# A two-branch sequence mixer on one core: the opening (input transposes, small vector loads, first TensorE work) and the step list are changed

## Chip, cores and metric

One core of a Trainium2 chip. The metric is the device time of one execution in microseconds: the median of the runs of the kernel. Durations below come from one profiled execution of the kernel before the change.

## What is computed

`x` is 2048 rows of 512. Two branches are computed from it and mixed by a gate per row.

```python
g = sigmoid((x * gate_w).sum(-1, keepdims=True))

# a: a diagonal complex state-space recurrence
dt = exp(log_dt);  Lam_bar = exp(dt * Lam);  B_bar = ((Lam_bar - 1) / Lam)[:, None] * Bmat
Bu = einsum("bld,pd->blp", x, B_bar)
h[t] = Lam_bar * h[t-1] + Bu[t]
a = 2 * einsum("blp,dp->bld", h, Cmat).real + x * Dskip

# b: linear attention with softmax features, 32 heads of 16
q, k, v = split(x @ wqkv)
phi(u) = concat(softmax(u @ w_phi), softmax(-u @ w_phi))
kv = sum_s phi(k)[s] v[s];  z = sum_s phi(k)[s]
b = (phi(q) kv) / (phi(q) z + 1e-6) @ wo

out = g * a + (1 - g) * b
```

## The kernel before

**The step list.** Each piece of work is a Python generator named by a short token, and every `yield` ends a part of it. The string `ORDER` (lines 24 to 53) is read token by token (lines 752 to 757): each token runs its generator up to the next `yield`. So `ORDER` is the order of instructions on TensorE, VectorE and ScalarE and of the late transfers on SyncE; each engine runs its own in that order and waits at the head of its list. `@5` names the PSUM bank that the part takes, `:D` gives an eviction to VectorE instead of ScalarE.

**The opening.** ScalarE's queue issues the load of the natural `Wk` block into `wk_nat` (the tile is named `C2r`, line 156), then `Wc` (157), then `Wv` (161). SyncE's queue issues five loads of 1 KB into the rows of `vec_n` (Lambda_im, Lambda_re, log_dt, Dskip, gate_w; line 159), then transposing loads of x tiles 0 to 7 (`x_load`, line 221), `Bn_r` and `Bn_i` (225, 226), eight transposing loads of `BrT`, `BiT` (228, 229), x tiles 8 to 15 and more. A DMA can be held at its issue by the landing of an earlier one.

**Steps that the prediction speaks of.** `W0` to `W3` (line 270) transpose `wk_nat` on TensorE and evict it; `f0` to `f3` (fold, line 372) multiply it with the block-diagonal `BD` made from `Wc` by `B` (305); each `f` reads all four `W`. `V` (278) transposes `vec_n` and copies it into `vec`, and GpSimd makes the diagonal `Dd` from its Dskip. `U`, `P`, `P2`, `P3`, `P4` work out the recurrence's magnitudes and angles from `vec` on VectorE and ScalarE; `i0` to `i3` (386) make sine and cosine tables `T2s`, `T2c` from them, with the temporaries `kk` and `psi` in the pool `tabtmp` (two buffers). `M` and `D` make the coefficient diagonals `dg`. `k`, `v`, `q` (418 to 436) are four products of 512 columns for one x tile each. `x`, `n`, `e`, `s` (features of two tiles: maximum, minimum, exponential, sum) run mostly on VectorE; `a0` to `a7` (507) add phi(k) times v into two PSUM banks and, with `gw_b` from `gw`, the gate's sum. `p`, `g`, `z`, `c`, `h`, `K` build the recurrence. At the end `X`, `N`, `E`, `S` make phi(q) for four tiles each and transpose it by DMA into `phT` (501), `o` (687) multiplies it with the summed state and sends `on` through a DMA transpose to `oT` (713), `y` (666) makes the recurrent output, and `t` (716) adds the projection, scales and stores it.

Of the kernel before, what the change touches and what calls it, by code (L numbers as in the profile page):

```python
# [10 lines left out]
ALU = mybir.AluOpType  # L11
AX = mybir.AxisListType
ACT = mybir.ActivationFunctionType
F32 = mybir.dt.float32
BF16 = mybir.dt.bfloat16
# [5 lines left out]
P = 128  # L21
MAGIC = 12582912.0
Z_MAX = 70.0
ORDER = """
B B W0@0 B V@1 V P W3@2 P W0:D W1@3 P2 W2@4 P2 P2 P2 U B W3 P2 gw P3 W1 W2 v1@5 U f1@6 P4 f2@7 P P4 P4 P2 f1 f0@1 P3
i0 U f2 f3@2 v0@0 i0 i1 f0 f3 i1 i0 i0 U i0 i2 i1 i1 v2@3 i2 i1 k2@4 i2 i3 k2 i2 k0@6 i3 k1@7 k1 i2 k0:D v0:D i3 M
v1:D x0 n0 n0 k3@1 k4@2 k5@4 i3 v2 k6@6 n0 k3 i3 v3@0 x0 x0 L x0 k7@7 k5 k4 D n0 x0 n0 v3 p20@5 p02@3 n1 x1 p00@1 e0
k6:D v7@4 p00 p20:D x1 n1 x1 v4@2 p32@0 x1 p22@6 x1 x2 v7 e0 x2 p10@1 p30@5 p12@4 s0 n1 v4 p10 s0 x2 p02 v6@2 p30 s0
x2 n1 v5@1 p22 p32 s0 g000@3 g101@5 n1 n2 s0 p12:D k8@6 k7 s0 e1 e1 k9@0 n2 x2 s0 k8 k9 g101 a0@74 n2 n2 x3 n2 g001@6
k11@0 e2 x3 s1 x3 n3 a0 x3 v6 v10@2 s1 n3 s1 e2 k11 n3 s1 g000 k12@0 D n3 g001 x3 s1 x4 s1 n3 g101 k13@5 k12 s1 n4 s2  # L30
s2 n4 x4 e3 a1 g000 x4 v5 n4 e3 x4 s2 g100@0 a1 n4 g011@3 s2 x4 k13 s2 s3 g100 s2 k10@1 n4 w1@5 g011 s2 g001 k10 s3 s3
a2 n5 n5 w0@6 x5 g100 w1 g010@1 e4 s3 n5 x5 s3 n5 g011 x5 x5 w2@0 s3 D v10 e4 s3 a2 k14@5 x5 g110@2 x6 g011 w0 g010
k15@3 w3@6 n5 a3 n6 s4 g010 k14 w2 e5 s4 v8@5 x6 s4 s4 g010 x6 a3 g111@0 v9@1 e5 z0 k15 s4 x6 g111 s4 g110 v9 c03@3
g110 s5 z0 v8 g201@1 g111 n6 c03 g111 c10@5 n6 n6 s4 a4 x6 g211@3 c02@0 w3 g110 c10 g210@6 z0 s5 z0 n6 g200@2 c13@5 z0
c02 n7 z0 e6 z0 q1@0 s5 z0 x7 s5 e6 x7 q1 g200 a4 n7 s5 c13 q0@0 n7 g201 x7 n7 x7 s5 v14@5 s6 x7 z1 g200 q0 v11@2 g201
z1 s5 q3@0 z1 s6 g210 q3 n7 z0 nA s6 z1 e7 s6 nA v11 c12@1 c12 z0 a5 v14 q2@0 xA z1 z1 xA e7 s7 s6 g210 c01@2 g211
c11@1 xA a5 g210 g211 v12@5 g211 s6 c11 z1 v13@6 z1 nA z2 xA z1 c01 z2 v13 nA s7 s6 g300@3 v12 g301@1 q11@2 z1 xA
c00@6 q2 c00 z2 g300 a6 nA eA xB xB eA s7 v15@5 s7 g311@0 g301 z2 xB g301 nB z2 g311 s7 g300 q7@6 s7 nB sA sA z2 a6
g310@1 g311 q15@3 nB q7 v15 g310 xB s7 xB nB a7 r0 g311 nB q11 g310 z2 sA g310 z3 eB z3 sA eB a7 z3 q5@6 q10@5 z3 q4@0
q15 q6@2 sA Y q8@1 sB h00@3 Y q10 sA z2 q5 h01@5 h00 h10@6 h01 h11@7 q9@3 sB q6 h11 z3 r1 sB q9 z2 q12@5 z3 h10 z2  # L40
q13@2 z3 z3 sA q4 sB z3 K1@7 G h20@3 sB sA r0 sB z3 h31@6 sB sA sA G q13 h20 h21@0 h31 h30@2 h21 Y q12 b0 r1 K0@3 sB
sB sB h30 END o0@6 K1 X1 K0 o0 Y N1 q8 y1@4 X1 o0@0 o0 o2@5 o2 X1 N1 q14@2 X1 o2@7 N1 b0 o0 N1 X1 q14 N1 X2 o1@3 o0 N2
b1 o1 y0@1 o0 G E1 o2 o2 K3@2 o1@6 b1 E1 G y0 N2 o1 r2 X2 o1 E1 E1 o1 K3 K2@0 X2 y1 o0 y0 o2 o3@3 o3 o3@5 y2@2 o3 t0
N2 o1 y2 o3 o1 N2 y3@6 S1 r3 X2 r3 S1 S1 K2 S1 y1 y2 S1 y4@0 X2 S1 o2 t1 o2 N2 o3 S1 y6@7 S1 y7@3 b2 y3 S1 r2 S1 X3 y4
E2 o3 b3 t2 N3 E2 t0 y4 E2 t1 y3 o4@1 E2 X3 b3 y6 y5@5 o3 S2 t2 S2 X3 S2 S2 o4 t0 o4@4 y7 o4 o4 y5 o4 o4 t1 o5@2 t2 o5
S1 X3 o5@1 o5 S1 t3 S2 N3 y7 y5 b2 S2 o5 y11@4 o5 t3 N3 o5 S2 N3 o6@2 o6 o6@6 o4 o5 o6 y6 o7@1 y11 S2 t4 S2 o6 o6 o7
t3 o6 o7@2 X3 y8@6 o7 o7 o6 t4 N3 E3 t5 o7 o7 y9@0 o8@1 y8 t4 o7 E3 t5:D y10@2 S2 E3 S2 o8 S2 o8@5 o8 o8 y9 t6 y11 o8
o8 E3 S3 o9@1 S3 o9 o9@5 t7 o9 t6 t6 o9 y9 t7 S3 S3 o9 o8 y14@7 o9 S3 y8 S3 o10@3 S3 o9 S3 o10 y10 y14 o10@1 t8 o10
o11@5 t5 S3 o10 o10 o11 t9 t8 t7 t9 o11@3 y14 o12@6 o12 o11 o10 S3 y12@1 o12@0 o11 o12 o12 o11 o12 y10 o10 S3 o13@5 S3
o11 o13 o12 y12 o13@6 t10 o13 y15@3 o11 o14@0 o13 t10:D y12 o14 o14@2 o13 y13@5 o14 y15 o12 o13 o15@6 o14 o14 t8 o15  # L50
o13 o15@0 o15 t11 o14 o15 y13 o14 t10 o15 t11 y15 o15 y13 t14 t11 o15 t13 t9 t14 t13:D t12 t12:D t14 t15 t15 t13 t12
t15
"""
TWO_PI_LO = float(np.nextafter(np.float32(2.0 * np.pi), np.float32(0.0)))
INV_2PI = float(1.0 / (2.0 * np.pi))
ACT_SET = "natural_log_exp_and_others"
# [9 lines left out]
def kernel(  # L66
# [18 lines left out]
    nc = tc.nc  # L85
# [13 lines left out]
    x2 = A_x[0]  # L99
# [9 lines left out]
    def bank(shape, dtype, name):  # L109
        return ps.tile(shape, dtype, tag=f"t{sel['banks'].pop(0)}", name=name, bufs=1)  # L110

    def evac(out_ap, in_ap):
        if sel["eng"] == "act":
            nc.scalar.copy(out=out_ap, in_=in_ap)  # L114
        else:
            nc.vector.tensor_copy(out=out_ap, in_=in_ap)
# [31 lines left out]

    man_g = tc.manual_schedule(engines={mybir.EngineType.PE, mybir.EngineType.DVE, mybir.EngineType.Activation, mybir.EngineType.SP})
    man_g.__enter__()  # L150
    vec_n = const.tile([20, P], BF16, name="vec_n")
    Wc = const.tile([P, HG, Dh], BF16, name="Wc")
    Wv = const.tile([P, KT, D], BF16, name="Wv")
    wk_nat = const.tile([P, KT, D], BF16, name="C2r")
    C2r = wk_nat
    nc.scalar.dma_start(out=wk_nat[:], in_=B_wqkv[:, D:2 * D].rearrange("(k p) n -> p k n", p=P))
    nc.scalar.dma_start(out=Wc[:], in_=B_w_phi.rearrange("(k hl) e f -> (hl e) k f", hl=8))
    for n, src in enumerate((A_Lambda_im, A_Lambda_re, A_log_dt, A_Dskip, gate_w)):
        nc.sync.dma_start(out=vec_n[4 * n:4 * n + 4, :], in_=src.rearrange("(j p) -> j p", p=P))
    pin_act_set()  # L160
    nc.scalar.dma_start(out=Wv[:], in_=B_wqkv[:, 2 * D:3 * D].rearrange("(k p) n -> p k n", p=P))

    xT = const.tile([P, KT, S], BF16, name="xT")
    Wo = const.tile([P, KT, D], BF16, name="Wo")
# [9 lines left out]
    RG = const.tile([P, NTI], F32, name="RG")  # L174
    ge = const.tile([P, NTI], F32, name="ge")
    hpi_t = const.tile([P, 1], F32, name="hpi_t")
    nc.vector.memset(hpi_t[:], float(np.pi / 2.0))
    C2i = const.tile([P, PT, D], BF16, name="C2i")
    C3r, C3i = Wk2, Wv
# [40 lines left out]
    def x_load(ti):  # L220
        nc.sync.dma_start_transpose(out=xT[:, :, ti * P:(ti + 1) * P], in_=x_res[ti // 4, ti % 4])

    for ti in range(8):
        x_load(ti)
    nc.sync.dma_start(out=Bn_r[:], in_=A_B_re.rearrange("(j p) d -> p j d", p=P))
    nc.sync.dma_start(out=Bn_i[:], in_=A_B_im.rearrange("(j p) d -> p j d", p=P))
    for kt in range(KT):
# [12 lines left out]
    fk = fk_g.__enter__()  # L240
    sk_g = tc.tile_pool(name="smallK", bufs=1, reuse_waits="tile")
    sk = sk_g.__enter__()
    tab_g = tc.tile_pool(name="tabtmp", bufs=2, reuse_waits="tile")
    tabp = tab_g.__enter__()
    iot = tabp.tile([P, NC], F32, name="iot", bufs=1)
    make_identity(nc, ident[:])
# [29 lines left out]
        yield  # L276

    def st_V():
        pvt = bank([P, 20], BF16, "pvt")
        nc.tensor.transpose(pvt[:], vec_n[:], ident[0:20, 0:20])  # L280
        yield
        nc.vector.tensor_copy(out=vec[:].rearrange("p n j -> p (n j)"), in_=pvt[:])
        nc.gpsimd.affine_select(out=Dd[:], in_=dsk.unsqueeze(2).to_broadcast([P, KT, P]), compare_op=ALU.is_equal,
                                fill=0.0, base=0, pattern=[[0, KT], [-1, P]], channel_multiplier=1)
        yield

    def st_U():
        VT(out=sq2, in0=lam, in1=lam, op=ALU.mult)
        yield
        VT(out=den_, in0=par[:, 4, :], in1=par[:, 5, :], op=ALU.add)  # L290
        yield
        nc.vector.reciprocal(out=den_, in_=den_)
        yield
        VS(out=den_, in0=den_, scalar1=2.0, scalar2=None, op0=ALU.mult)
        yield
# [43 lines left out]
    def st_gw():  # L339
        nc.vector.tensor_copy(out=gw_b[:], in_=vec[:, 4, :])  # L340
        yield
# [208 lines left out]

    def st_c(dst, j):
        d_, da, db = ((C2r, DG_BR, DG_NBI), (C2i, DG_NBI, DG_NBR))[dst]
        pc = bank([P, D], F32, "pc")
        MM(out=pc[:], lhsT=dg[:, da, j, :], rhs=CrT[:, j, :], start=True, stop=False)
        MM(out=pc[:], lhsT=dg[:, db, j, :], rhs=CiT[:, j, :], start=False, stop=True)
        yield
        evac(d_[:, j, :], pc[:])
        yield
# [33 lines left out]
    def st_h(j, ri):  # L592
        U1 = uv[j][:, 0]
        prev = slice(ZP - 1, ZP - 1 + NC)
        da, db = ((DG_MR, DG_NMI), (DG_MI, DG_MR))[ri]
        ph = bank([P, NC], F32, "ph")
        MM(out=ph[:], lhsT=ident[:], rhs=U1[:, ri, :], start=True, stop=False)
        MM(out=ph[:], lhsT=dg[:, da, j, :], rhs=H3[:, j, 0, prev], start=False, stop=False)
        MM(out=ph[:], lhsT=dg[:, db, j, :], rhs=H3[:, j, 1, prev], start=False, stop=True)
        yield  # L600
        evac(H1[:, j, ri, :], ph[:])
        yield

    def st_G():
# [111 lines left out]
    def st_t(n):  # L716
# [8 lines left out]
        else:  # L725
# [4 lines left out]

    small1, big1 = (lambda: sk), (lambda: fk)
    small3, big3 = (lambda: pools["sq"][1]), (lambda: pools["eq"][1])
    st = {"V": st_V(), "U": st_U(), "P": st_P(), "P2": st_P2(), "P3": st_P3(), "P4": st_P4(), "B": st_B(), "gw": st_gw(),
          "M": st_M(), "D": st_D(), "L": st_L(), "G": st_G(), "Y": st_Y(), "END": st_END()}
    for j in range(4):
        st.update({f"W{j}": st_W(j), f"f{j}": st_f(j), f"w{j}": st_w(j), f"i{j}": st_i(j), f"z{j}": st_z(j), f"r{j}": st_r(j),
# [54 lines left out]
```

## Time and profile before

| what | us |
| --- | --- |
| runs shown | 173.09, 172.84, 173.07 |
| median | 173.07 |
| profiled execution, its own time | 173.42 |
| its span in the profile | 171.7 |
| TensorE busy, 1049 products | 157.8 |
| VectorE busy | 144.2 |
| ScalarE busy | 116.9 |
| first transpose of `W` (waits for `wk_nat`) | 4.74 |
| `V` on TensorE / copy to `vec` on VectorE | 5.57 / 5.78 |
| first table pass `i0` on VectorE | 8.86 |
| first product of `v` | 8.96 |
| first product of `k` | 14.35 |

The span runs from the first to the last recorded instruction; the execution's own time has 1.7 us more around it. Busy time of TensorE counts products that overlap in its pipeline, so the pace is read from the distances between starts. In a timeline line the columns are start, duration, engine, line, operation, output from input, shapes and count; several like instructions are merged into one. In a windows line they are the stretch, its length, busy time and count of each engine, granted clock, the DMA engines' share and GB/s.

### The profile page before, as it was taken

What the parts mean: (1) busy time and instruction counts of PE and PEld (TensorE: products, weight loads), DVE (VectorE), ACT (ScalarE), POOL (GpSimd) and SP (SyncE); (2) the same over time, 40 slices, a digit from 0 to 9 for tenths busy, and PEclk for the clock granted to TensorE, in tenths of its full rate; (3) what the DMA queues carried; (4) which work ended last, traced back from release to release, by engine and by line L of the source; (5) the groups of instructions that cost most, each with busy time, mean ns of one, the idle gap of its engine ahead of it and who ended that gap; (6) DMA issues with size and microseconds to landing.
All of it is one profiled execution on the core that took longest, in us unless ns stands there. A gap on an engine that the chain in (4) does not pass through costs nothing.

```text
span 171.7 us, 2969 instructions
## 1 busy us (share of the span) xinstructions
PE 157.8 (92%) x1049; PEld 80.5 (47%) x1069; DVE 144.2 (84%) x349; ACT 116.9 (68%) x239; POOL 5.3 (3%) x23
## 2 busy tenths in 40 slices
PE   0599989999999999999999999999999998998991
PEld 0354456455455454444545444545455543444540
DVE  3775999999999999999999999999999958335411
ACT  2559799988789587586687698896864394251311
POOL 3223000000000000000000000000000000000000
PEclk9999999999999999999999999999999999999999
DMA  5945974554546000000000008341178458596443
GB/s 126 208 106 157 265 96 92 95 116 100 92 95 164 20 0 2 0 4 0 0 0 4 0 0 168 76 33 34 33 183 203 85 145 183 134 174 154 122 138 106
DMA packets 50710, 15.94 MB, mean 93 GB/s; under 512 B 46088, under 2 KB 50696, under 8 KB 50696
## 3 DMA queue, kind: packets, MB, share of 16 engines
q1 hardware_dynamic: 49112, 14.70, 39.9%
q10 hardware_dynamic: 1584, 1.07, 2.6%
q8 instruction: 8, 0.13, 0.3%
q14 instruction: 6, 0.05, 0.1%
HBM read 2.64 MB, written 2.10 MB: 28 GB/s over the span
## 4 chain that ended last, share of the span: by engine, by line
PE 63%; DVE 18%; DMA 11%; ACT 3%; SPq 2%; issue 1%
PE pq L415 8%; PE py L675 6%; PE py L676 6%; PE py L720 6%; PE pgq L538 6%; PE pgq L541 6%; PE pv L415 5%; DMA phT<-EEq 4%; DVE smk L450 3%; DVE mxk L450 3%; PE py L682 2%; DMA xT<-in_A_x_dram 2%; DVE mnk L450 2%; DMA C2r<-in_B_wqkv_dram 2%; PE pk L645 2%; DMA oT<-on 2%
## 5 line engine op out<-in xcount | busy, mean ns | idle before, releaser
L415 PEld LDWEIGHTS <-xT 128*128 128x128 bf16 x192 | 18.4, 99 | 22.7 <-DMA xT<-in_A_x_dram 2.1
L133 ACT ACTIVATE EEk<-EEk 128x1024 bf16<-128x1024 bf16 x20 | 20.9, 1072 | 2.5 <-DVE EEk L466 2.5
L707 DVE SCALAR_TENSOR_TENSOR on<-pn,RG,rd 128x256 bf16<-128x256 f32 x32 | 14.4, 478 | 9.2 <-ACT rd L133 9.2
L133 ACT ACTIVATE ld<-pn 128x16 f32<-128x16 f32 x32 | 5.5, 185 | 18.4 <-PE pn L698 18.1
L415 PE MATMUL pv<-Wv,xT 128*128 128x512 bf16 x62 | 16.3, 400 | 1.9 <-DMA xT<-in_A_x_dram 1.8
L541 PE MATMUL pgq<-xT,LBT 128*128 128x512 bf16 x63 | 16.0, 379 | 0.1
L720 PE MATMUL py<-Wo,oT 128*128 128x512 bf16 x61 | 15.6, 379 | 0.2
L415 PE MATMUL pq<-Wq,xT 128*128 128x512 bf16 x63 | 15.2, 379 | 0.1
L415 PE MATMUL pk<-Wk,xT 128*128 128x512 bf16 x63 | 15.2, 379 | 0.1
L133 ACT ACTIVATE EEq<-EEq 128x1024 bf16<-128x1024 bf16 x12 | 12.2, 1047 | 1.3 <-DVE EEq L466 1.3
L676 PE MATMUL py<-Wv,H 128*128 128x512 bf16 x32 | 12.1, 379 | 0.1
L114 ACT CAST uv<-pgq 128x512 bf16<-128x512 f32 x16 | 9.3, 582 | 3.9 <-PE pgq L546 2.8
L724 ACT ACTIVATE ot<-py,G 128x512 bf16<-128x512 f32 x12 | 8.2, 682 | 5.5 <-PE py L720 4.9
L676 PE MATMUL py<-C2i,H 128*128 128x512 bf16 x31 | 11.7, 379 | 0.1
L675 PE MATMUL py<-C2r,H 128*128 128x512 bf16 x31 | 11.7, 379 | 0.1
L675 PE MATMUL py<-Wk,H 128*128 128x512 bf16 x31 | 11.7, 378 | 0.0
L114 ACT CAST Xq<-pq 128x512 bf16<-128x512 f32 x16 | 9.3, 589 | 3.4 <-PE pq L415 3.3
L698 PEld LDWEIGHTS <-phT 128*128 128x128 bf16 x128 | 7.0, 98 | 7.1 <-DMA phT<-EEq 2.7
L450 DVE TENSOR_TENSOR smk<-smk 128x512 bf16<-128x512 bf16 (+2 forms) x30 | 9.9, 330 | 0.2
L486 DVE TENSOR_TENSOR EEk<-EEk,rck 128x2048 bf16<-128x2048 bf16 x8 | 9.7, 1218 | 0.0
L541 PEld LDWEIGHTS <-LBT 128*128 128x128 bf16 x64 | 6.2, 98 | 7.3
L579 DVE TENSOR_TENSOR_SCAN w<-ssm_par,ut 128x512 bf16<-128x512 f32 x8 | 9.6, 1215 | 0.0
(169 smaller groups left out, 339.4 us busy)
## 6 DMA issues: line engine op xcount, KB each, us to landing
out_dram<-ot SPq DMA_DIRECT2D x16, 128.0 KB, 2.1
C2r<-in_B_wqkv_dram ACTq DMA_DIRECT2D x1, 512.0 KB, 3.9
Wv<-in_B_wqkv_dram ACTq DMA_DIRECT2D x1, 512.0 KB
Bn_r<-in_A_B_re_dram SPq DMA_DIRECT2D x1, 512.0 KB, 4.6
Bn_i<-in_A_B_im_dram SPq DMA_DIRECT2D x1, 512.0 KB
Wo<-in_B_wo_dram SPq DMA_DIRECT2D x1, 512.0 KB
xT<-in_A_x_dram SPq DMA_TRANSPOSE x16, 3.5
oT<-on SPq DMA_TRANSPOSE x16, 2.3
```

The lines of the kernel that those rows point to most:

```text
L114: nc.scalar.copy(out=out_ap, in_=in_ap)
L133: ins = nc.scalar.activation(**kw)
L415: MM(out=pt[:], lhsT=xT[:, kt, ti * P:(ti + 1) * P], rhs=W[:, kt, :], start=(kt == 0), stop=(kt == KT - 1))
L450: VT(out=t[:], in0=cur[:, :, :, 0:n, :], in1=cur[:, :, :, n:2 * n, :], op=op)
L486: VT(out=E5, in0=E5, in1=rc[:].to_broadcast([P, L, 2 * NB, Dh, 4]), op=ALU.mult)
L538: MM(out=pgq[:], lhsT=BT[:, kt, js], rhs=xT[:, kt, r1 * NC:(r1 + 1) * NC], start=(kt == 0), stop=False)
L541: MM(out=pgq[:], lhsT=LBT_[:, kt, js], rhs=xT[:, kt, (r1 - 1) * NC:r1 * NC], start=False, stop=(r1 == 1 and kt == KT - 1))
L579: nc.vector.tensor_tensor_scan(out=w[:, ri, :], data0=rb, data1=ut[:, ri, :], initial=0.0, op0=ALU.mult, op1=ALU.add)
L675: MM(out=py[:], lhsT=src[:, j, 0, off:off + P], rhs=cr[:, j, :], start=(j == 0), stop=False)
L676: MM(out=py[:], lhsT=src[:, j, 1, off:off + P], rhs=ci[:, j, :], start=False, stop=False)
L707: nc.vector.scalar_tensor_tensor(out=on[:, 2 * hf:2 * hf + 2].rearrange("p g h e -> p (g h) e"), in0=pns[hf][:, :, 0:Dh], scalar=RG[:, ti: ...
L720: MM(out=py[:], lhsT=oT[:, g, :], rhs=Wo[:, g, :], start=False, stop=(g == HG - 1))
```

## The change

SyncE's queue opens with the eight x transposes; the vector loads leave it. Lambda_im, Lambda_re and log_dt go to ScalarE's queue, behind `Wk` and ahead of `Wc` and `Wv`, into a tile of 12 rows; Dskip and gate_w go into a tile of 8 rows, loaded by SyncE behind x tile 7. `V` is split to match: `V` for the first three, `V2` for the other two and `Dd`. TensorE opens with nine products of 128x512 of a tile `fillw` that VectorE fills with ones; their bank (`t7`) is read by nobody. `tabtmp` has three buffers instead of two. `ORDER` is another list of the same tokens plus two `V2`. Two options, `C2_VECTOR` and `H1_VECTOR`, are added empty, so they change nothing.

```diff
 ORDER = """
-B B W0@0 B V@1 V P W3@2 P W0:D W1@3 P2 W2@4 P2 P2 P2 U B W3 P2 gw P3 W1 W2 v1@5 U f1@6 P4 f2@7 P P4 P4 P2 f1 f0@1 P3
-i0 U f2 f3@2 v0@0 i0 i1 f0 f3 i1 i0 i0 U i0 i2 i1 i1 v2@3 i2 i1 k2@4 i2 i3 k2 i2 k0@6 i3 k1@7 k1 i2 k0:D v0:D i3 M
...
+V@0 W1@1 V B U P P W1 P2 P2 P W0@2 W2@3 B P2 P2 W3@4 W3 P2 B v2@5 P4 P4 W0:D P4 P3 v1@6 W2 i0 B U P2 f0@7 P3 i2 f1@0
+f3@1 U i1 f2@4 f0 i0 f3 f1 i2 f2 U i0 v3@3 i0 i1 v5@2 i0 i1 k1@7 v3:D M i1 k1 k0@1 i1 i2 k2@0 i2 k0:D k5@4 i3 v4@3 v1
...
-    vec_n = const.tile([20, P], BF16, name="vec_n")
+    vec_n = const.tile([12, P], BF16, name="vec_n")
+    vec_m = const.tile([8, P], BF16, name="vec_m")
...
     nc.scalar.dma_start(out=wk_nat[:], in_=B_wqkv[:, D:2 * D].rearrange("(k p) n -> p k n", p=P))
+    for n, src in enumerate((A_Lambda_im, A_Lambda_re, A_log_dt)):
+        nc.scalar.dma_start(out=vec_n[4 * n:4 * n + 4, :], in_=src.rearrange("(j p) -> j p", p=P))
     nc.scalar.dma_start(out=Wc[:], in_=B_w_phi.rearrange("(k hl) e f -> (hl e) k f", hl=8))
-    for n, src in enumerate((A_Lambda_im, A_Lambda_re, A_log_dt, A_Dskip, gate_w)):
-        nc.sync.dma_start(out=vec_n[4 * n:4 * n + 4, :], in_=src.rearrange("(j p) -> j p", p=P))
+    nc.scalar.dma_start(out=Wv[:], in_=B_wqkv[:, 2 * D:3 * D].rearrange("(k p) n -> p k n", p=P))
     pin_act_set()
-    nc.scalar.dma_start(out=Wv[:], in_=B_wqkv[:, 2 * D:3 * D].rearrange("(k p) n -> p k n", p=P))
...
+    fillw = const.tile([P, 512], BF16, name="fillw")
+    nc.vector.memset(fillw[:], 1.0)
+    spin = ps.tile([P, 512], F32, tag="t7", name="spin", bufs=1)
+    for _ in range(9):
+        nc.tensor.matmul(out=spin[:], lhsT=fillw[:, 0:P], rhs=fillw[:], start=True, stop=True)
     nc.vector.memset(hpi_t[:], float(np.pi / 2.0))
...
     for ti in range(8):
         x_load(ti)
+    for n, src in enumerate((A_Dskip, gate_w)):
+        nc.sync.dma_start(out=vec_m[4 * n:4 * n + 4, :], in_=src.rearrange("(j p) -> j p", p=P))
     nc.sync.dma_start(out=Bn_r[:], in_=A_B_re.rearrange("(j p) d -> p j d", p=P))
...
-    tab_g = tc.tile_pool(name="tabtmp", bufs=2, reuse_waits="tile")
+    tab_g = tc.tile_pool(name="tabtmp", bufs=3, reuse_waits="tile")
...
     def st_V():
-        pvt = bank([P, 20], BF16, "pvt")
-        nc.tensor.transpose(pvt[:], vec_n[:], ident[0:20, 0:20])
-        yield
-        nc.vector.tensor_copy(out=vec[:].rearrange("p n j -> p (n j)"), in_=pvt[:])
+        pvt = bank([P, 12], BF16, "pvt")
+        nc.tensor.transpose(pvt[:], vec_n[:], ident[0:12, 0:12])
+        yield
+        nc.vector.tensor_copy(out=vec[:, 0:3, :].rearrange("p n j -> p (n j)"), in_=pvt[:])
+        yield
+
+    def st_V2():
+        pvt = bank([P, 8], BF16, "pvt")
+        nc.tensor.transpose(pvt[:], vec_m[:], ident[0:8, 0:8])
+        yield
+        nc.vector.tensor_copy(out=vec[:, 3:5, :].rearrange("p n j -> p (n j)"), in_=pvt[:])
         nc.gpsimd.affine_select(out=Dd[:], in_=dsk.unsqueeze(2).to_broadcast([P, KT, P]), compare_op=ALU.is_equal,
```

In the part of the list not shown, the first `k` comes behind `v2`, `v1`, the four `f`, `v3` and `v5` (before: behind `v1`, the four `f`, `v0` and `v2`); `V2` comes between `p10` and `p12`, and `gw` between the first `g` steps, ahead of `a0`. Seven early evictions were VectorE's (`W0`, `k0`, `v0`, `v1`, `k6`, `p20`, `p12`), five are now (`W0`, `v3`, `k0`, `k4`, `v7`); of the last step `t` four were (5, 10, 12, 13), six are now (5, 8, 9, 10, 13, 14).

## The prediction

> **What bounds the kernel now.** First I read the busy row of each engine in the page, then the shares of the chain that ended last.
>
> ```profile
> PE   0599989999999999999999999999999998998991
> DVE  3775999999999999999999999999999958335411
> PEclk9999999999999999999999999999999999999999
> ...
> PE 63%; DVE 18%; DMA 11%; ACT 3%; SPq 2%; issue 1%
> ```
>
> TensorE is full from the third slice (4.3 us each) to the end, VectorE from the fifth to the 32nd. So the kernel is held by TensorE's amount of work, with VectorE almost level, and only time in which TensorE waits or runs slowly can be won. How much is that? The code has 632 products of 512 columns: 192 in `k`, `v`, `q`; 144 in `g`; 16 in `c`; 24 in `h`; 32 in `K`; 160 in `y`; 64 in `t`. Late in the chain twelve of them (from 98.65 us) take 2.59 us, 0.216 each: 136.5 us. The small ones add 17.7 (sixteen steps of `a` at 0.33, 16 of `o` at 0.26, 32 products of `p` at 0.11, 84 of 128 columns at 0.054 in `W`, `f`, `w`, `K`, `y`): 154.2. All but the first 0.9 us of it lies between 8.96 us (first `v`) and 168.22 (last product of `t` in the chain): 159.3 us for 153.3 of work. So 6.0 us are lost there, besides the 8.96 ahead of it. The timeline of TensorE at the start shows where much of that is:
>
> ```profile
> 8.96 1.89 PE L415 MATMUL pv<-Wv,xT 128*128 128x512 bf16 x4 [1.82 <-DMA xT<-in_A_x_dram]
> 10.64 1.91 PE L375 MATMUL pf<-BD,Xq 128*128 128x128 bf16 x16
> 12.35 2.16 PE L415 MATMUL pv<-Wv,xT 128*128 128x512 bf16 x8
> 14.35 0.38 PE L415 MATMUL pk<-Wk,xT 128*128 128x512 bf16 x1
> ```
>
> Starts give the pace. Four `v` products fill 8.96 to 10.64, 0.42 each; sixteen `f` products fill 10.64 to 12.35, 0.107 each; the next eight fill 2.00 us, which is one more at 0.42 and seven at 0.22. The array is at half pace until about 12.8, 3.8 us after the first `v`, though the granted-clock row says full all along. Then the waits:
>
> ```profile
> PE pv L415 <- DMA xT<-in_A_x_dram: 1.8, 1, 1.8
> DVE kk L388 <- ACT T2c L139: 3.0, 1, 3.0
> PE pn L698 <- DMA phT<-EEq: 1.4, 2, 0.8
> ```
>
> ```profile
> SPq L221 <- DMA C2r<-in_B_wqkv_dram: 0.8, 1, 0.8
> ```
>
> (microseconds, times, longest): TensorE waits 1.8 us for x; VectorE stands 3.0 us at the third table `i2`, whose `kk` buffer ScalarE still reads; `o` waits 1.4 us for phi; SyncE waits for Wk. Last, the DMA engines' share in single microseconds (last two figures: share, GB/s):
>
> ```profile
> 3.00:4.00 1.00, 0.00 (x0) 0.00 (x0) 0.34 (x2) 0.09 (x1) 0.00 (x0) 1.00 0.99 333
> ...
> 7.00:8.00 1.00, 0.14 (x2) 0.00 (x0) 0.90 (x9) 0.98 (x3) 0.00 (x0) 1.00 1.27 258
> 8.00:9.00 1.00, 0.04 (x1) 0.04 (x2) 0.90 (x8) 1.00 (x1) 0.40 (x2) 1.00 1.12 203
> 9.00:10.00 1.00, 1.00 (x3) 0.39 (x4) 1.00 (x3) 0.49 (x2) 0.42 (x1) 1.00 0.45 100
> ```
>
> They are full until 9 us and half idle after.
>
> **The change part by part.** *x ahead on SyncE's queue.* Five vector issues (0.78 to 2.57) leave; x0 moves from 2.60 to 0.78. But Wk, Wv and the x tiles share full engines, about 1.5 MB to 9 us (sum of the GB/s by microsecond), and the first `v` is now `v2`, the third tile: Wk, Wv and three x tiles are 1.4 MB, so bandwidth puts it at about 8.5. There is also a hold: x1 was issued at 4.71, when Wk landed (4.70), and the wait row names Wk. In issue order Wk, four vectors, Wc, the fifth vector and x0 stand before x1: it is the ninth, waiting for the first. In the new program Wk, three vectors and Wc (ScalarE) and x0, x1 (SyncE, 1.27 each) come before Wv, which is about the eighth, and x2 is about the ninth and waits for Wk. Wk now shares with x0, so it lands at 4.7 to 5.3; x1's landing took 4.2 from its issue, so x2 lands at 8.9 to 9.5 if held, 7.5 to 8.5 if not. First `v`: 8.3 to 9.5; I take 8.9, a gain of 0.0. The two vectors left on SyncE (0.6 us) come behind x7, and Bn_r still leaves about 2 us earlier than at 13.80.
>
> *Vectors behind Wk on ScalarE's queue.* Three issues at 0.3 push Wc from 1.24 to about 2.1 and Wv from 2.51 to 2.7 to 3.0; ScalarE idles 2.9 us there (its first exponential waits for `vec`), so the issues are free. The last vector landed at 5.57 before; now it stands behind Wk, at 4.8 to 6.3: I take +0.4 us. Behind it in TensorE's list wait all four `W` (2.1 us as before), done by 8.4 at worst, and `f` now follows two `v`; VectorE's chain `P`, `P2`, `P4` to the first table starts 0.4 later, plus up to 0.6 for three `B` (0.28 each) that used to precede it.
>
> *Nine products of a constant tile.* The fill by VectorE is not in the trace; between a 128x8 memset (0.07) and a 128x512 pass (0.42), covered by the 1.81 us that VectorE idles before `B`. Products 9 x 0.42 = 3.8 us, from about 1.3 to 5.1: 4.74 us of TensorE idle time covers them, and what runs past it eats the 1.8 us before the first `v`. What they can buy is the half pace: 4 x 0.20 in `v`, 16 x 0.053 in `f`, one more 0.20: 1.9 us. Bounds 0 (pace lost again or never gained) and 1.9. I take 1.9: nine at half pace last as long as half pace lasted in this trace.
>
> The Trainium skill (TensorE: Matmul & The Clock Gate, Part 1) has a free-running window of about 3.4 us of activity that lifts the gate, and an idle one that shuts it; by that 3.8 us is only just enough, and the sum could be 0 here as well as 1.9.
>
> *Third `tabtmp` buffer.* The 3.0 us wait of `i2` goes. Two passes of `i2` (0.49 + 0.75) and some of the rest move into VectorE's hole; ScalarE's eviction of `f`, which delayed the sine, is still there. VectorE gains 1.2 to 2.7, less 0.4 to 1.0 for its later start: I take 1.2.
>
> *The list.* Work per engine is the same (one transpose and one 0.15 copy more; of the early evictions VectorE does five instead of seven). I added the rows along both lists: TensorE work ahead of `a(n)` minus VectorE work up to the end of the normalising pass it needs. Before: -3.5, -5.0, -6.0, -4.9 for n = 0 to 3; after: -3.8, -2.7, -2.7, -1.6. So VectorE may fall some 2 us behind its old place except at `a0`, where 0.3 less room and a TensorE that gained 0.7 more than VectorE cost up to 1.0; half a microsecond of slack was there (normalised 33.5, `a0` 34.2), so I take +0.3. At the `phT` waits the same difference goes from -8.6 to -3.7 at `o8`, -4.2 to -4.0 at `o13`: of the 1.4 us I count 0.3 won, bounds 0 and 1.4. From each `o` to its `t` lie at least 5.0 us of TensorE work (5.5 before); logarithm, exponential, two products and the `oT` transfer take about 4.7 (0.2 + 0.2 + 0.9 + 3.4), so they stay hidden; what came later than 0.3 us would be lost microsecond for microsecond.
>
> Sum: 0.0 - 1.9 + 0.3 - 0.3 = -1.9. The profiled execution took 173.42 (span 171.7 and 1.7 around it), so 171.5; the median shown is 0.35 lower: **171.2**.
>
> **Rivals.** *A, the half pace stays.* The pre-heated array cools between 5.1 and 8.9, or the nine don't suffice. For it: the transposes of `W` at 4.74 to 7.13 did nothing for the pace at 8.96. Against: no row shows TensorE losing pace after a pause, but none is long enough to. Time: 173.1, within 172.5 and 173.6 by the list's share.
>
> The same page (Part 4) says that transposes don't count as activity; by that rule the gap 5.1 to 8.9 is idle, 3.8 us against a window of 3.4, which speaks against the change; a third of this rival's chance rests on it.
>
> *B, slower: Wv is held.* If two x more stand ahead in the order, Wv (or Wc, or the third vector) becomes the ninth or tenth DMA and waits for Wk or x0, landing at 4.7 to 5.3, instead of leaving at 2.7. A 512 KB load took 3.9 (Wk) to 4.6 (Bn_r), so it lands at 8.6 to 9.9, and the pause is long enough that the pace may be lost too: up to +0.9; a held third vector delays VectorE's whole chain by 1 to 2 and, VectorE being full to 133 us, the end. It decides from a landing of Wv at 10.8, where 1.9 us are used up. Time 173.07 + 0.9 = 174.0 (173.5 to 175). For it: the hold of x1. Against: at 0.3 us each ScalarE's six issues are out before the third x.
>
> *C, more than that.* The stall of `phT` goes as well (another 1.1) and x2 is not held (0.6): 169.6.
>
> **How the numbers follow.** Forecast 0.55 (its own range 170.3 to 172.2), A 0.20, B 0.17, C 0.08. The range runs from C's upper part to B's nearer part, 169.8 to 173.9, leaving out about 0.14. What 0.2% can tell from no change is 172.7 to 173.4: faster 0.55 + 0.08 + 0.04 of A = 0.67, same 0.11 of A, slower 0.17 + 0.05 of A = 0.22.
>
> **What would show it.** Four `v` products from the first start spaced 0.22, `f` at 0.054 (clock); first `v` near 8.9 and its releaser (x or Wv); Wk's landing by 5.3; the `vec` copy near 6.2; no `kk` wait for `T2c`; `a0` waiting under 0.5 us. Wrong: spacing 0.42 at the first `v`, an ACT-queue DMA waiting for x0, or TensorE idle over 1 us more than before after 14 us.

## The result, and the profile after

| | runs | median us | range | ratio to before, 95% |
| --- | --- | --- | --- | --- |
| before | 4 | 173.02 | 172.84 to 173.09 | |
| after | 4 | 174.91 | 174.73 to 175.76 | 1.0114 [1.0083, 1.0145] |

The change makes the kernel 1.9 us slower. The profiled execution of after took 175.07 (span 173.3), that of before 173.42: 1.65 of the 1.9 lie between the two traces and can be traced. In the tables of this document a run counts as slow when it lies over 1.5% above the fastest of its kernel: three of ten of e5, its profiled one among them, and two of six of e3, which the ratios leave out and the medians and ranges hold.

The page of after, with the same rows as before:

```profile
PE   6229999999999999999999999999999999999891
DVE  4049599999999999999999999999999948835221
PEclk9956999999999999999999999999999999999999
...
PE 83%; DMA 9%; SPq 4%; DVE 1%; issue 1%; ACT 0%; ACTq 0%
```

TensorE is nearly empty in the second and third slice (4.3 us each), VectorE empty in the second, and the granted clock drops in the third and fourth. From the fifth slice on TensorE is fuller than it was: it now carries 83% of the chain instead of 63%. So the loss lies ahead of 17 us, and behind it something was won. The timeline of ScalarE's queue shows the cause:

```profile
0.78 0.42 ACTq L159 DMA_DIRECT2D C2r<-in_B_wqkv_dram  x1
1.23 0.69 ACTq L161 DMA_DIRECT2D vec_n<-in_A_Lambda_im_dram  x1
1.96 0.26 ACTq L161 DMA_DIRECT2D vec_n<-in_A_Lambda_re_dram  x1
6.12 0.26 ACTq L161 DMA_DIRECT2D vec_n<-in_A_log_dt_dram  x1
7.72 0.41 ACTq L162 DMA_DIRECT2D Wc<-in_B_w_phi_dram  x1
8.17 0.59 ACTq L163 DMA_DIRECT2D Wv<-in_B_wqkv_dram  x1
```

log_dt stands 3.9 us at the head of the queue before it is issued, `Wc` another 1.3 us, and `Wv`, which went out at 2.51 before, goes out at 8.17. What ended `Wc`'s wait is in the chain of waits in order of time (start, duration, what):

```profile
3.43 4.27 DMA xT<-in_A_x_dram
8.17 4.81 DMA Wv<-in_B_wqkv_dram
13.03 3.44 PE pv L432 x8
```

x2's transfer lands at 7.70 and `Wc` is issued at 7.72; `Wv` goes right behind it, takes 4.81, and the first `v` starts. TensorE's timeline and waits to the first `k` (18.92, before 14.35):

```profile
8.56 0.18 PE L290 MATMUL pvt<-ident,vec_n 12*128 12x12 bf16 x1 [3.04 <-DMA vec_n<-in_A_log_dt_dram]
8.67 1.28 PE L283 MATMUL ptw<-ident,C2r 128*128 128x128 bf16 x16
13.03 3.44 PE L432 MATMUL pv<-Wv,xT 128*128 128x512 bf16 x8 [3.07 <-DMA Wv<-in_B_wqkv_dram]
16.30 1.06 PE L392 MATMUL pf<-BD,Xq 128*128 128x128 bf16 x16
17.41 1.67 PE L432 MATMUL pv<-Wv,xT 128*128 128x512 bf16 x7
```

```profile
PE pv L432 <- DMA Wv<-in_B_wqkv_dram: 3.1, 1, 3.1
PE pvt L290 <- DMA vec_n<-in_A_log_dt_dram: 3.0, 1, 3.0
...
PE py L753 <- DMA oT<-on: 0.4, 1, 0.4
```

The `W` transposes start at full pace (16 in 1.28, where e4 below takes 1.07 at full pace and e6 1.89 at half), the eight `v` behind the next gap run at half (0.38 to 0.43 each), `f` at full again. The waits for `phT`, `dg` and `EEk`, 2.4 us together before (1.4, 0.7, 0.3), are gone; 0.4 for `oT` is all that is left behind the first `k`.

**The balance of the two executions**, by starts: first `v` +4.07 (8.96 to 13.03); from there to the first `k` +0.50 (5.39 to 5.89); from there to the end of the execution -2.92 (159.07 to 156.15). Sum +1.65. In the second term after does 16 `v` where before did 12, 0.86 more of work at full pace; so the pace gave -0.36. In the third, those 0.86 are work no longer to be done, and of the other -2.06 the waits that went make up 2.0.

### The profile page after: what moved, and what is told of

Its sections match the earlier page's. It is cut to its first block, busy times and chain, and to the rows that moved or that the text cites. A ratio compares the mean times of both kernels' runs of the same rounds, so it can differ in the third digit from the quotient of the medians.

```text
span 173.3 us, 2996 instructions
## 1 busy us (share of the span) xinstructions
PE 160.4 (93%) x1059; PEld 80.9 (47%) x1079; DVE 143.5 (83%) x351; ACT 115.1 (66%) x239; POOL 7.0 (4%) x23
## 3 DMA queue, kind: packets, MB, share of 16 engines
q10 hardware_dynamic: 1608, 1.07, 2.4%
## 4 chain that ended last, share of the span: by engine, by line
PE 83%; DMA 9%; SPq 4%; DVE 1%; issue 1%; ACT 0%; ACTq 0%
PE pv L432 9%; PE pq L432 8%; PE pk L432 8%; PE pgq L558 8%; PE pgq L555 8%; PE py L753 7%; PE py L708 6%; PE py L709 6%; PE py L715 3%; DMA oT<-on 3%; DMA Wv<-in_B_wqkv_dram 3%; DMA xT<-in_A_x_dram 2%; PE kvacc L530 2%; PE pk L677 2%; PE pk L678 2%; PE pn L731 2%
## 5 line engine op out<-in xcount | busy, mean ns | idle before, releaser
L432 PE MATMUL pv<-Wv,xT 128*128 128x512 bf16 x61 | 17.2, 409 | 3.2 <-DMA Wv<-in_B_wqkv_dram 3.1
L753 PE MATMUL py<-Wo,oT 128*128 128x512 bf16 x63 | 16.1, 379 | 0.6 <-DMA oT<-on 0.4
L432 PE MATMUL pq<-Wq,xT 128*128 128x512 bf16 x62 | 15.8, 379 | 0.2
L757 ACT ACTIVATE ot<-py,G 128x512 bf16<-128x512 f32 x10 | 6.8, 678 | 10.7 <-PE py L753 7.2
L709 PE MATMUL py<-Wv,H 128*128 128x512 bf16 x32 | 12.1, 379 | 0.0
L708 PE MATMUL py<-Wk,H 128*128 128x512 bf16 x32 | 12.1, 379 | 0.0
L135 ACT ACTIVATE EEq<-EEq 128x1024 bf16<-128x1024 bf16 x12 | 11.6, 1040 | 0.0
L759 DVE TENSOR_SCALAR ot<-py,G 128x512 bf16<-128x512 f32 x6 | 4.4, 748 | 6.7 <-PE py L753 5.7
```

The source lines that it names most:

```text
L135: ins = nc.scalar.activation(**kw)
L432: MM(out=pt[:], lhsT=xT[:, kt, ti * P:(ti + 1) * P], rhs=W[:, kt, :], start=(kt == 0), stop=(kt == KT - 1))
L708: MM(out=py[:], lhsT=src[:, j, 0, off:off + P], rhs=cr[:, j, :], start=(j == 0), stop=False)
L709: MM(out=py[:], lhsT=src[:, j, 1, off:off + P], rhs=ci[:, j, :], start=False, stop=False)
L753: MM(out=py[:], lhsT=oT[:, g, :], rhs=Wo[:, g, :], start=False, stop=(g == HG - 1))
```

## The experiments

In the compiled program every DMA names one of eight completion counters, in turn, in an order worked out across both queues; the DMA that takes a counter again waits at its issue until the one that had it has landed. In before that order begins Wk, four vectors, Wc, gate_w, x0, then x1 (waits for Wk) and Wv (for the first vector). In after it is Wk, x0 to x3, Lambda_im, x4, Lambda_re, then x5 (waits for Wk), **log_dt (waits for x0)**, x6, **Wc (waits for x2)**, x7, Wv (waits for Lambda_im, but stands behind Wc in its queue). The traces bear the order out: x1 left at 4.71 in before, when Wk had landed (4.70), and `Wc` at 7.72 in after, when x2 had (7.70). When x0 landed in after isn't in the trace, so that log_dt waited for x0 rests on the order and on e1. My theory: this hold is the whole loss, because the first `v` sets the time. Rivals: what costs is the later `vec` and with it VectorE's chain; or TensorE's own part (pace, list) is at fault. Each kernel was timed beside runs of before on the same chip; these had medians of 172.84 (e1 to e4), 172.64 (e5 to e8) and 172.83 (e9 to e11).

| label | edit | median us | range | ratio to before, 95% |
| --- | --- | --- | --- | --- |
| e1_x2_behind_wv | after, hold taken away by order alone | 171.36 | 170.29 to 171.90 | 0.9907 [0.9875, 0.9938] |
| e2_before_spin | before + nine products | 172.67 | 172.01 to 173.59 | 0.9994 [0.9972, 1.0017] |
| e3_one_spin | after, one product for nine | 176.27 | 174.94 to 178.02 | 1.0166 [1.0119, 1.0213] |
| e4_vec_on_sp | after, vectors on SyncE ahead of x0 | 170.25 | 170.12 to 170.52 | 0.9856 [0.9834, 0.9879] |
| e5_late_wv | e4, `Wv` alone held | 171.61 | 169.53 to 174.28 | 0.9905 [0.9869, 0.9942] |
| e6_late_vec | after, vectors alone held | 173.82 | 172.99 to 175.15 | 1.0080 [1.0051, 1.0108] |
| e7_before_spin_tab3 | e2 + third `tabtmp` buffer | 171.47 | 170.80 to 172.56 | 0.9936 [0.9909, 0.9962] |
| e8_vec_on_sp_one_spin | e4, one product for nine | 172.61 | 171.39 to 173.39 | 1.0004 [0.9979, 1.0029] |
| e9_vec_on_sp_again | e4 once more | 170.80 | 170.24 to 171.22 | 0.9887 [0.9865, 0.9908] |
| e10_v1_first | e4, x1's `v` ahead of x2's | 170.39 | 169.82 to 170.56 | 0.9856 [0.9834, 0.9877] |
| e11_fill | e4 + eight products in the gap | 169.55 | 169.14 to 170.90 | 0.9838 [0.9804, 0.9873] |

### The hold: e1 and e4

e1 asks the program's order to put x2 behind `Wv` (an order, not a wait), which changes who takes which counter; e4 moves the three vectors to SyncE's queue, ahead of x0. Both do the same work as after.

```diff
-    nc.scalar.dma_start(out=Wv[:], ...)
+    wv_dma = nc.scalar.dma_start(out=Wv[:], ...)
...
+        if ti == 2:
+            order_after(ld, wv_dma, "x2 behind Wv in issue order")
```

```diff
     for n, src in enumerate((A_Lambda_im, A_Lambda_re, A_log_dt)):
-        nc.scalar.dma_start(out=vec_n[4 * n:4 * n + 4, :], ...)
+        nc.sync.dma_start(out=vec_n[4 * n:4 * n + 4, :], ...)
```

> Same queues and the same order on each queue as the changed kernel; only the order in which the DMAs take the eight completion counters differs (x2 is ordered behind Wv, so log_dt, Wc and Wv no longer take a counter that an x transpose holds). Theory H (the hold is the loss): log_dt, Wc and Wv are issued by 3.2 us instead of 6.12, 7.72 and 8.17, V runs before 6.5, the first v at 8.5 to 9.6 instead of 13.03, time 170.5 to 172. Rival C (x shares full DMA engines with Wk and Wv, so the landings are late in any order): issues early but V after 8 and first v after 11.5, time above 174. Rival L (the new list itself is slower): first v near 9 and time still 173 or more.

> The changed kernel with the three vector loads on SyncE's queue ahead of x0, as before; Wc and Wv are then sixth and eighth to take a counter and wait for nothing. Theory H: Wv issued by 2.7, x0 at about 1.7, first v 8.5 to 9.5, time 170.5 to 172, within 0.5 of the run with x2 behind Wv. Rival C: between that and the changed kernel, as x still shares the engines. Rival L: 173 or more with a first v near 9.

e1's queue of ScalarE, from the third vector on:

```profile
2.27 0.46 ACTq L161 DMA_DIRECT2D vec_n<-in_A_log_dt_dram  x1
2.75 0.44 ACTq L162 DMA_DIRECT2D Wc<-in_B_w_phi_dram  x1
3.22 0.53 ACTq L163 DMA_DIRECT2D Wv<-in_B_wqkv_dram  x1
```

Nothing is held on ScalarE's queue any more, and `Wv` leaves 5 us earlier than in after; on SyncE's queue x2 now waits 1.5 us for Wk. TensorE's timeline of e1:

```profile
7.23 0.17 PE L292 MATMUL pvt<-ident,vec_n 12*128 12x12 bf16 x1 [1.70 <-DMA vec_n<-in_A_log_dt_dram]
7.33 1.89 PE L285 MATMUL ptw<-ident,C2r 128*128 128x128 bf16 x16
9.01 2.84 PE L434 MATMUL pv<-Wv,xT 128*128 128x512 bf16 x8
```

The first `v` starts at 9.01, the first `k` at 14.31, and after's loss becomes a gain: 174.91 to 171.36. One part of the expectation fails: `V` runs at 7.23 and not before 6.5, since log_dt, 1 KB issued at 2.27, is there only then. In e4 `Wv` leaves at 1.80 and TensorE's timeline reads:

```profile
5.16 0.18 PE L290 MATMUL pvt<-ident,vec_n 12*128 12x12 bf16 x1
5.27 1.07 PE L283 MATMUL ptw<-ident,C2r 128*128 128x128 bf16 x16
8.27 3.53 PE L432 MATMUL pv<-Wv,xT 128*128 128x512 bf16 x8 [1.94 <-DMA xT<-in_A_x_dram]
```

The first `v` waits for its x tile, no longer for `Wv`. The first `k` is at 14.26 against 18.92, 4.66 earlier, and the median, 170.25 against 174.91, is 4.66 lower. That the two agree so exactly is chance: e9, the same program as e4, has its first `k` 5.95 earlier than after and a median 4.1 lower. The pace of the first eight `v` is half in after and in e4, so it doesn't make this difference. The theory stands: with the order alone changed (e1) the loss is gone. The two kernels say more: without the hold the rest of the change is worth 1.5 us (e1) to 2.6 (e4; 2.0 in e9).

### Which of the held loads: e5 and e6

e5 is e4 with `Wv` ordered behind x6, so that it inherits x0's counter; e6 is after with `Wc` and `Wv` ahead of the vectors and x1 ordered behind `Wv`, which holds the vectors alone.

```diff
+        if ti == 6:
+            order_after(wv_dma, ld, "Wv behind this x in issue order")
```

```diff
     nc.scalar.dma_start(out=wk_nat[:], ...)
+    nc.scalar.dma_start(out=Wc[:], ...)
+    wv_dma = nc.scalar.dma_start(out=Wv[:], ...)
     for n, src in enumerate((A_Lambda_im, A_Lambda_re, A_log_dt)):
...
+        if ti == 1:
+            order_after(ld, wv_dma, "x1 behind Wv in issue order")
```

> The run with vectors on SyncE's queue, but Wv alone takes its counter behind x6, so that it waits for x0 (issued at about 6 instead of 1.8 us); vectors and Wc as there. Theory P (TensorE's first v sets the time): first v near 11 instead of 8.27, time about 170.3 + 2.7 = 173.0. Theory D (the vectors' arrival and with it VectorE's chain sets the time): the later v is caught up while TensorE would wait for VectorE anyway, time under 171.3.

> The changed kernel with Wc and Wv ahead of the vectors on ScalarE's queue; Wv is on time (issued by 2.5 us), log_dt waits for x1, so that V runs at 8.5 to 9.5, and the first v behind V and the four W at 10.5 to 11. Theory P: about 170.3 + 2.5 = 172.8, like the run with Wv late. Theory D: VectorE starts 3.5 to 4 us later than with the vectors on SyncE's queue, 173.5 to 174.5, near the changed kernel's 174.9 though v starts 2 us sooner than there.

TensorE's timeline, e5 and then e6:

```profile
10.13 3.57 PE L435 MATMUL pv<-Wv,xT 128*128 128x512 bf16 x8 [3.45 <-DMA Wv<-in_B_wqkv_dram]
```

```profile
10.02 0.17 PE L292 MATMUL pvt<-ident,vec_n 12*128 12x12 bf16 x1 [4.93 <-DMA vec_n<-in_A_log_dt_dram]
10.11 1.89 PE L285 MATMUL ptw<-ident,C2r 128*128 128x128 bf16 x16
11.79 3.35 PE L434 MATMUL pv<-Wv,xT 128*128 128x512 bf16 x8
```

In e5 `Wv` leaves at 5.95 with `vec` nearly as early as in e4 (5.68 against 5.37); first `v` 1.9 later, median 0.8 to 1.4 more than e9 and e4. The median, 171.61, lies between the two forecasts, the interval overlaps those of e4 and e9, and the profiled execution (173.28) is among the longest of runs that scatter widely. The granted clock orders them: the two with a mean of 1.00 took 169.53 and 170.04, the five with 0.99 took 171.27 to 171.84 (3.4 us at half clock, as in the last section, lower the mean over 170 us by 0.01). So what e5 shows of a late `Wv` can't be told from the pace lost in the gap that it leaves.

In e6 `vec` is there only at 10.22, 1.4 us later than in after, and yet e6 is faster (173.82 against 174.91, first `k` 17.60 against 18.92). Its time lies in the range forecast for theory D, but the trace speaks for P: what is behind the first `k` takes as long, 155.8 in e6, 156.0 in e4, 156.15 in after. So in these executions a late start of VectorE's chain adds nothing there: late vectors cost because `V` stands at the head of TensorE's list, ahead of the sixteen `W` and the first `v`. By the medians late vectors alone cost 3.0 to 3.6 us against e9 and e4, clear of noise; that a late `Wv` alone costs isn't shown. After has both.

### The nine products: e2, e3, e8

```diff
-    for _ in range(9):
-        nc.tensor.matmul(out=spin[:], lhsT=fillw[:, 0:P], rhs=fillw[:], start=True, stop=True)
+    nc.tensor.matmul(out=spin[:], lhsT=fillw[:, 0:P], rhs=fillw[:], start=True, stop=True)
```

This is e3 (on after) and e8 (on e4); e2 adds `fillw` and the nine to before.

> The kernel before with the fill and the nine constant products alone. If the pace is kept over the wait for x: the first four v spaced 0.22, f at 0.054, and up to 1.9 us less, 171.1 to 172.2 (VectorE may hold some back). If the array cools between the transposes of W and the first v: v spaced 0.42, f 0.107 and 173.0 plus or minus 0.3.

> The changed kernel with one constant product instead of nine. Theory H: the pace was lost before the first v anyway (0.42 there), so nothing but the transposes of W slows (0.08 to 0.107 each, 0.4 us, hidden behind the wait for Wv): 174.9 plus or minus 0.3. If the nine cost something (their place ahead of V): down to 174. If they gave something: up to 175.5.

> The run with vectors on SyncE's queue with one constant product instead of nine. There the pace was lost again before the first v (0.42 to 0.44 there), so 170.3 plus or minus 0.3 if the nine give nothing; 0.5 to 1.5 more if they give something outside the first v (transposes of W, or an earlier return of the pace).

e2: `v` 0.22 apart, first `k` 12.12 instead of 14.35, so the pace is there, and the time is the same (0.9994). In the profiled execution (172.33) half of the 2.2 us is given back: `dg` makes TensorE wait 1.5 instead of 0.7, `phT` 1.7 instead of 1.4. The median mixes two cases. Four of e2's twelve runs have a mean granted clock of 0.990, as if the clock had fallen once, and took 172.88 to 173.59; the other eight (0.997 to 1.000) have a median of 172.2, 0.6 below before. So each forecast of e2 describes some of its runs. In e7's execution the waits that take the place are others again:

```profile
PE pv L420 <- DMA xT<-in_A_x_dram: 2.0, 1, 2.0
PE pn L703 <- DMA phT<-EEq: 1.7, 2, 0.9
PE spin L181 <- DVE fillw L178: 1.5, 1, 1.5
PE pk L420 <- DMA xT<-in_A_x_dram: 1.4, 1, 1.4
PE pl L531 <- DMA Bn_i<-in_A_B_im_dram: 0.7, 1, 0.7
```

e3 settles nothing: its runs lie in two groups (174.9 to 175.3 and 177.2 to 178.0), none of its forecasts has its median, and its interval overlaps that of after. e8 is clear: without the nine, e4 loses 1.8 (against e9) to 2.4 us, more than either forecast. Its timeline:

```profile
5.03 1.89 PE L282 MATMUL ptw<-ident,C2r 128*128 128x128 bf16 x16
8.17 3.59 PE L431 MATMUL pv<-Wv,xT 128*128 128x512 bf16 x8 [1.25 <-DMA xT<-in_A_x_dram]
11.55 1.91 PE L391 MATMUL pf<-BD,Xq 128*128 128x128 bf16 x16
```

`W` and `f` take 1.9 instead of 1.1 and the first `k` comes 0.83 later than in e4; 0.9 more is waits for `oT` (1.6 against 0.7). What makes up the rest stays open.

### The list and the third buffer: e7

```diff
-    tab_g = tc.tile_pool(name="tabtmp", bufs=2, reuse_waits="tile")
+    tab_g = tc.tile_pool(name="tabtmp", bufs=3, reuse_waits="tile")
```

> The kernel before with the nine products and the third table buffer, its list kept. If the list makes the gain of the run with vectors on SyncE's queue (170.25): 172.0 to 172.7 here, at most 0.5 under the run with the nine products alone. If the buffer makes it: 170.3 to 171.3, and no wait of a kk pass for T2c.

The ratio is 0.6% under e2's, and the intervals don't overlap: the buffer (`kk` no longer waits for `T2c`, 1.2 us in e2) is worth about 1 us with the old list; the median, 171.47, lies between the two forecasts. From the first `k` to the end the profiled executions with the old list took 159.1 (before), 160.2 (e2) and 160.3 (e7), those with the new one 155.8 to 158.3, after 156.15. 0.86 of that is moved work; where the first `k` comes at about the same time (14.35 in before, 14.31 in e1, 14.26 in e4) the waits are 0.6 to 2.2 less. Two of the waits can be put down to one part: e2's 1.5 for `dg` is gone in e7, with the buffer alone, while 1.7 for `phT` stays there and is 0.4 at most in every execution with the new list. The new list with two buffers was not tried, so list and buffer are not told apart further.

### What bounds the repaired kernel: e9, e10, e11

e9 is e4 unchanged; e10 changes two tokens; e11 adds eight products of `fillw` behind the `W` transposes.

```diff
-... W3 P2 B v2@5 P4 P4 W0:D P4 P3 v1@6 W2 ...
+... W3 P2 B v1@6 P4 P4 W0:D P4 P3 v2@5 W2 ...
```

```diff
-... W3@4 W3 P2 B v2@5 ...
+... W3@4 F W3 P2 B v2@5 ...
...
+    def st_F():
+        for _ in range(8):
+            MM(out=spin[:], lhsT=fillw[:, 0:P], rhs=fillw[:], start=True, stop=True)
+        yield
```

> The same program as e4_vec_on_sp once more, to see whether its time repeats beside the two kernels below. Theory (the hold of Wc and Wv by the completion counters was the whole loss, and the new list is worth 2 to 3 us behind the first k): 170.0 to 171.0, first v near 8.3, first k near 14.3, the profiled execution's own time some 156 above its first k. If e4's time was a lucky session: 171.5 or more.

> e4's program with the v products of the second x tile put before those of the third in TensorE's list. In e4 the first v waited 1.9 us for its tile, and the second tile lands earlier. Theory 1 (the first v starts as soon as its tile is there, and a gap under 1 us after the W transposes keeps the pace): first v near 7.0 to 7.6 and its products 0.22 apart, first k 2 to 3 us earlier than in e4: 167.5 to 169.0. Theory 2 (the start moves, the pace is lost all the same): first k 0.7 to 1.2 us earlier, 169.0 to 169.8. Theory 3 (the second v or f waits instead, for its own tile or for the tables): first k where it was, 170.0 to 171.

> e4's program with eight more products of the constant tile between the W transposes and the first v. Theory 1 (TensorE loses its pace in the gap between the transposes and the first v, and work in the gap keeps it): first v near 8.3, its products 0.22 apart, first k some 1.5 to 1.7 us earlier than in e4: 168.5 to 169.0. Theory 2 (the pace isn't set by what runs in that gap): products of v still 0.43 apart, first v later by what runs past x (up to 1.7 us if the added ones run at half pace): 170.3 to 172.

TensorE's timeline of e9, of e10 and of e11:

```profile
5.58 1.74 PE L283 MATMUL ptw<-ident,C2r 128*128 128x128 bf16 x16
8.29 1.90 PE L432 MATMUL pv<-Wv,xT 128*128 128x512 bf16 x8 [0.97 <-DMA xT<-in_A_x_dram]
12.97 3.62 PE L432 MATMUL pk<-Wk,xT 128*128 128x512 bf16 x16
```

```profile
7.62 1.90 PE L432 MATMUL pv<-Wv,xT 128*128 128x512 bf16 x8 [0.62 <-DMA xT<-in_A_x_dram]
12.10 1.04 PE L432 MATMUL pv<-Wv,xT 128*128 128x512 bf16 x4 [0.82 <-DMA xT<-in_A_x_dram]
12.97 3.62 PE L432 MATMUL pk<-Wk,xT 128*128 128x512 bf16 x16
```

```profile
6.48 1.89 PE L297 MATMUL spin<-fillw 128*128 128x512 bf16 x8
8.63 1.90 PE L437 MATMUL pv<-Wv,xT 128*128 128x512 bf16 x8 [0.27 <-DMA xT<-in_A_x_dram]
12.99 3.62 PE L437 MATMUL pk<-Wk,xT 128*128 128x512 bf16 x16
```

e9's time repeats e4's within 0.6 us, but its execution kept the pace that e4's lost, with the same instructions, so its first `k` comes 1.3 us sooner than expected. e10 starts `v` 0.67 earlier than e9 and gains nothing at the first `k`, since a later x tile lands at 12.1 (its third theory). e11 keeps the pace and is the fastest kernel measured: 169.55, between its two forecasts, though its interval still overlaps those of e4, e9 and e10. That the pace makes e11's gain isn't shown. The mean granted clock is 0.998 or more in all six runs of e11 and 0.988 to 0.990 in four of the six of e9, which speaks for the eight products keeping the clock from falling; but e9's two runs whose clock did not fall took 170.60 and 171.22, no less than the others.

All three have the first `k` at 13.0, and from there to the end they take 158.3, 157.0 and 156.4; e9's waits show where:

```profile
PE py L753 <- DMA oT<-on: 1.8, 3, 1.1
...
PE pf L392 <- DMA H<-in_B_wqkv_dram: 0.7, 1, 0.7
```

With the first `k` at 13.0 the `f` of the Wq block waits 0.7 us for SyncE's late loads and `y` waits 1.8 for `oT` (0.7 in e4), so in these executions a shorter opening doesn't pay in full: e9's first `k` is 1.3 us ahead of e4's, and its execution is 1.0 us longer (171.22 against 170.25).

## Why the prediction was wrong

**The step that failed** is in the first part: "In the new program Wk, three vectors and Wc (ScalarE) and x0, x1 (SyncE, 1.27 each) come before Wv, which is about the eighth, and x2 is about the ninth and waits for Wk." The mechanism was read rightly from x1's hold before. The count was made by the times at which the issues would leave if nothing held them. The counters go by the program's own order, in which x0 to x3 and not one or two x tiles stand ahead of Lambda_im, and six ahead of log_dt; that makes log_dt the tenth DMA, Wc the twelfth, Wv the fourteenth. From there on the forecast's numbers fall in a row: vectors at "4.8 to 6.3" (V at 8.56), Wv leaving at "2.7 to 3.0" (8.17), first `v` "8.3 to 9.5; I take 8.9, a gain of 0.0" (13.03, a loss of 4.07). The vectors' time was too early even without the hold: `V` ran at 7.23 in e1.

Rival B names this very mechanism, the third vector or `Wc` waiting for x0, and was given 0.17 because "at 0.3 us each ScalarE's six issues are out before the third x". That argument assumes what was to be shown, that the order is the order in time. Its size was also too small: it held one load, landing at 8.6 to 9.9; the trace has three waits in one queue, one behind the other (log_dt for x0, `Wc` for x2, `Wv` behind `Wc`), and `Wv` lands at 12.98. The rival's time, 173.5 to 175, does hold the measured 174.91, though by other terms.

**The nine products**: -1.9 forecast, -0.36 between the two profiled executions. They do raise the pace (`W` in 1.28), and a gap behind them loses it again, as rival A had it. The gap is the 3.0 us in which `V` waits for log_dt: the granted clock falls at 9.36, before the last `W` (9.65) and the 3.1 us gap ahead of `v`, and it stays low through that second gap until 16.20. In e4's execution it falls at 8.20, at the end of a gap of 1.94 us.

**The list and the buffer**: +0.3 for `a0` and -0.3 for `phT` forecast, -2.0 measured in waits (2.4 to 0.4). No `a0` wait came. The sum along the lists compared TensorE's lead with VectorE's work at `a0` to `a3` and had no term for the waits for `dg` (0.7) and `EEk` (0.3); `dg`'s goes with the 3.0 us hole of `kk` in e7, and for `EEk`'s I take the same cause without a test. At `phT` "bounds 0 and 1.4" held the answer, and 0.3 was the wrong end.

**In the sum**: forecast 0.0 - 1.9 + 0.3 - 0.3 = -1.9; by the traces +4.07 - 0.36 - 2.06 = +1.65. (The small products ahead of that sum add up to 17.5 by the figures given there, not 17.7; nothing hangs on it.) Right were x1's hold as a sign, the sign of error ("an ACT-queue DMA waiting for x0"), the first `v` without a hold (forecast 8.3 to 9.5; 8.27 in e4, 9.01 in e1), and the time without it (forecast 171.2; e1 171.36, e4 170.25). The last is partly luck: a clock term that was too large and a list term that was too small cancel.

## What to carry to other kernels

A DMA's place in the queue isn't its only order. Where the program hands out a fixed number of completion counters in turn, count every DMA of every queue in the order in which the program takes the counters, and for each one past that number look up whose landing it waits for; a 1 KB load that draws the counter of a slow transposing load stops all that stands behind it in its own queue. When several small loads are moved behind big ones, the queue that pays is the one that they join.

What products that only warm the array are worth depends on what follows: the nine are worth nothing in the median of e2, where their pace is lost in some runs and in others partly given back where the next transfer or engine is due, and 1.8 to 2.4 us in e4, of which the traces place 0.8 ahead of the first `k`.

## What was not expected of the hardware

**The granted clock falls and rises in steps of one length.** The windows of after and then of e4 in single microseconds (the third figure from the end is the granted clock):

```profile
9.00:10.00 1.00, 0.96 (x14) 0.80 (x12) 0.00 (x0) 1.00 (x1) 0.00 (x0) 0.68 1.18 154
10.00:11.00 1.00, 0.00 (x0) 0.00 (x0) 0.03 (x1) 0.76 (x3) 0.00 (x0) 0.50 0.74 184
...
16.00:17.00 1.00, 1.00 (x15) 0.81 (x14) 1.00 (x4) 0.28 (x1) 0.92 (x3) 0.90 1.06 365
```

```profile
8.00:9.00 1.00, 0.73 (x2) 0.28 (x3) 1.00 (x5) 0.99 (x3) 0.00 (x0) 0.60 0.36 82
...
11.00:12.00 1.00, 1.00 (x10) 0.51 (x8) 0.99 (x3) 0.00 (x0) 0.92 (x2) 0.69 0.56 121
```

A clock of 0.68 in a microsecond that falls from 1 to 0.5 puts the fall at 9.36; 0.90 in one that rises puts the rise at 16.20: 6.84 us at half. In e4 the fall is at 8.20 and the rise at 11.62: 3.42 us, half of that. The Trainium skill (TensorE: Matmul & The Clock Gate, Part 1) states a free-running window of 3413 ns, and the two traces agree with it: one window and two. Counted back by 3.42 from e4's fall, a window of it ends at 4.78, just where its products become faster. In all four runs of after the mean granted clock is 0.979 to 0.980, which is what 6.84 us at half make of 173. If the window's place against the program differs from one execution to the next, that explains why e4 and e9, one program, show two paces. That reading was not tested by itself.

**Transposes on TensorE seem to count as activity.** The Trainium skill (TensorE: Matmul & The Clock Gate, Part 4) says that they don't. In e9 the sixteen `W` transposes from 5.58 take 1.74 us, between 1.07 at full pace and 1.89 at half, so some 13 of them run at half and the rise is at about 7.0. The 3.42 us ahead of it hold 2.0 us of products and 1.4 of transposes. In e1 the pace had not risen by 9.01 although one window, counted back from the rise inside its eight `v` (about 10.9), held 2.6 us of products. If products alone counted, 2.0 would have been enough and 2.6 not. e10 says the same: its sixteen `W` take 1.43, which puts the rise at about 6.3, and the 3.42 us ahead of it hold no more than the 2.6 us of products that did not do in e1, and 0.8 of transposes. This is worked out from three executions and not settled by them.

**The granted clock reads 1.00 before its first fall, whatever the pace**: the products of the opening that start 0.40 to 0.43 apart (the first seven of the nine in every profile that has them, and the first four `v` of before) lie in windows of 1.00. So that row, and a run's mean clock, tell of a fall and not of a pace that hadn't yet risen, as in e1.
